# Middle tiles of the key-value sums: from zero-padded full-height products to half-height products inside the projection blocks

## The chip, the cores and the metric

One Trainium2 chip, one NeuronCore. The metric is device time in microseconds (us) of one execution of the whole program. The program does a linear-attention layer and a soft mixture of experts behind it, all in 32-bit floats, in one launch.

## The reference

```python
# attention: batch 8, heads 8, sequence 576, head width 64, 128 features
proj = einsum('bhsd,df->bhsf', x, w_phi)              # x is q or k
proj = proj - max(abs(proj), axis=-1)
phi  = concatenate([exp(proj), exp(-proj)], axis=-1)
kv  = einsum('bhsf,bhsd->bhfd', k_p, v)               # sums over the 576 tokens
z   = sum(k_p, axis=2)
out = einsum('bhsf,bhfd->bhsd', q_p, kv) / (einsum('bhsf,bhf->bhs', q_p, z) + 1e-06)
# soft MoE: x is the attention output as (4608, 512); 32 slots, 8 experts of 4
logits = x @ phi
d = exp(logits - logits.max(0)) / column sums;  slot_input = d.T @ x
slot_out[e] = relu(slot_input[e] @ w1[e]) @ w2[e]
c = exp(logits - logits.max(1)) / row sums;     y = c @ slot_out
```

`kv` and `z` are made together: the kernel gives each row of `v` a 65th column of ones, so that one product gives the 64 columns of `kv` and the column `z`.

## The kernel before, in words

**Units and tiles.** The work of attention is cut into 32 units (`NU`). A unit is one head of a pair of batches: 2 x 576 = 1152 tokens, which make 9 tiles of 128 tokens (`NT`). 576 is four and a half tiles, so tile 4 of each unit, the middle tile, holds the last 64 tokens of one batch in its rows 0 to 63 and the first 64 of the other in rows 64 to 127. The two batches need separate sums.

**Projection blocks.** The tiles of all units in a row are cut into 72 blocks of 4 tiles (`NB`). `proj(b)` (matmuls of line 271) projects the keys of block b into the PSUM tile `psk` and the queries of block b-2 into `psq`. The head width is 64, so each of these matmuls uses 64 rows of the array; key and query products lie in different halves of the rows and alternate in the program: four of each, with 64 x 128 weights and 128 moving columns.

**Behind a projection.** DVE takes the largest absolute value of each key row (`kmax`, line 276), ACT makes two factors of it (`kfac`) and the exponentials `kf` (lines 302 and 305), POOL multiplies `v` with the factors into `vs` (`vals`, line 291). `kvmm` (line 318) then sums `kf` x `vs` over the tiles of a unit into the PSUM tile `kvp`, which has one buffer; its shape is two signs (`pn`) x two batches x 65 columns. Each matmul has 128 rows and 64 weight columns, two of them side by side in the two halves of the array's columns. `kvcopy` (line 327) takes `kvp` out of PSUM. `num` (line 371) multiplies the query exponentials with it, with the same 128 x 64 weights and 65 moving columns; DVE and POOL finish the quotient.

**The middle tile before.** The host stores 10 tiles of `v` for each unit: tile 4 comes twice, once with rows 64 to 127 zero and once with rows 0 to 63 zero. The four matmuls of tile 4 in `kvmm` move 130 columns, both copies, and so add into the sums of both batches at once (`m = 130 if t == 4`, lines 313 to 318). The zero rows keep the batches apart. `place` says where a tile stands in `vs`.

**The rest.** After every head group the tiles of attention output are transposed (line 741), logits are made (line 424) and running slot sums updated. At the end come the two expert layers (lines 848 and 943) and the output (lines 972 to 976). Their weights are 64 tiles of 512 KB, loaded into slots of 4096 bytes per partition. `room` works out how many slots fit beside the working buffers: 26 from the start, and then 29, 35, 38, 40 and 46 as working buffers are closed. The 64 - 46 = 18 last weights go to slots whose first weight has been used.

**The order.** All instructions of the first part are put down by hand, in the order of the string `ORDER`: one letter per task ("c" a projection block, "m" a piece of `kvmm`, "a" and "b" loads), each engine executing its own tasks in that order. `Plan.run` gives a buffer to each task as it comes. All loads and stores are issued by SP, in order; an issue that waits for a free buffer holds up those behind it.

Of the kernel before, what the change touches and what calls it, by code (L numbers as in the profile page):

```python
# [17 lines left out]
FE = 128  # L18
# [6 lines left out]
VW = 10 * 65  # L25
# [19 lines left out]
BUFS = {'xs': 3, 'kf': 3, 'vs': 2, 'vt': 2, 'qf': 3, 'un': 2, 'xT': 4, 'xc': 2}  # L45
PICK = {'xcopy': 'adda', 'kvcopy': 'daad', 'zcopy': 'ada', 'zlt': 'aadaa', 'zde': 'a'}
TOP = 196700


def room(bufs):  # L50

    parts = [bufs["xs"] * XW * 4, bufs["kf"] * 4096 + bufs["vs"] * 2624 + bufs["vt"] * 2624,
             bufs["qf"] * 4096 + 2 * 1056 + 512, bufs["un"] * 2368, (bufs["xc"] + 1) * G * DM * 4]
    return [int(n) // 4096 for n in np.cumsum([TOP - bufs["xT"] * 2048 - sum(parts)] + parts)]


class Plan:
# [42 lines left out]
ORDER = (  # L100
    "abbccdeafdebgbehiejefechigcjdklfmbgdnoelhimjfajkegmhijcpnoclfdmqlrhisgmfjktharujnovmvkbdicnogpcjdwmgwflrjhirqvaw"
    "mxfysbkrkdtnomlhizvnocAwgpvjcjwflmdqbrAArvkshimnoltfwckvdgnojrwfrgdkyjahimzlhivnocwqvpcgbdjmgdflrAfwAhimsjklnotr"
    "hiyAmkcjvnopgwcjbdavmxgzflArdqjmwlAfaAkvrwhisynorhizmtkgcjnovvjpwcblfxdmAqrwAAfsrkgmvhitlnojwkvchwajnoyrblrdiqmv"
    "vgwkzjcdpwfmdrgynoAsrfjkmhilAathiznoAcgvjcvblfxAwmxqdAAwrgpkjsfmnolhirtvmvkwdnorwghijrvyzmAcpjwvcwAbflxyAhrazfAd"
    "imkAlgBnojdBqcCgCjsBbBdatmlCkvjwrnoChirvgfjmhiDkpAnocEwFvcwkflmbhrxqxdimGgsnojBflBtCaxchCjykdiBnozBgCfjmvhwrClpr"
    "vdimDwgvkjwnocEFcblqadHxHIrJIKksfKnoltLmqyAdAgAhirfjmgkhicpjnovscbfvxtwmlwrzflAhrvAAdimwgvhyjrwkdiajrnozvgkmjvcp"
    "nowwcAblfyhAmzqdirlgmkjsfAahrxtnoxmjkvdicAnovApwAgcGlfjhwmlqrJdirfvgmkwjsknoradnotbchijvywcblfxgvmxqjdrwpdhimvgr"
    "kzwAsmkMgylftrnozLAhiAcnojvcbdjawmglfAvrqApjwmkshiArfvtnowmdkMyNvhirwgljrvnojmvczwwpcyAblaAzArdkAlmfAnoBhiBgCcjC"
    "fkdBqdBmCgfjshinoajrlxCAbmktDphivvnocwEgwjclfFrbqrvdmwgBsfBkmktCCjdhiBvnoOajBhiyxCcClrwflrnovNzdmkwhiDgnojpcEqvG"
    "wcFblgsHHrItdmyKIjfzlhiKAdkaxALgmAnoqvJrfMjmgvkwhiwAscnoApctblAxdrjGrgvfwmkdhilrgjvajmvkwnoOPfrjNnomvhicwwPpycyz"  # L110
    "bdkAlmfdgrnojzqJmlAajhixsAfrAOhimtkcnovvpwcgbdjlmgfrwqjdrvAklaAmhixwjnosfchitgmkvbjfxwrlxhrpyvnowmkvczdiAnowqcdy"
# [938 lines left out]
```

## Time and profile before

| what | us |
|---|---|
| three runs of the kernel | 341.21, 337.5, 337.83 (median 337.83) |
| span of the profiled execution | 339.8 |
| PE busy in it | 326.0 |
| DVE, ACT, POOL busy | 243.8, 234.5, 168.3 |
| granted TensorE clock, mean | 0.992 |
| read and written | 63.60 MB, 9.44 MB |

PE is the matmul engine; PEld is the load of its weights, which runs beside the matmuls. Each 32-bit matmul of the program appears twice in the trace, as two passes, each with its own weight load: 1152 matmuls of `num` give 2304 records. Shapes such as "128*64 128x65" are the rows and columns of the array that an instruction uses, then what it moves. The start times of the records tell the rate at which the passes follow each other; their durations (some 0.22 to 0.3 us) hold the way through the array too, so they overlap.

### The profile page before, as it was taken

To read this page: it belongs to the slowest core of one execution; us is meant where nothing else is said; L and a number is where in the kernel's file an instruction comes from. 1 tells how busy PE (TensorE), PEld (TensorE's weight loads), DVE (VectorE), ACT (ScalarE), POOL (GpSimd) and SP (SyncE) were. 2 spreads that over 40 slices of the span, in tenths; PEclk is the share of its full clock that TensorE was granted. 3 is DMA by queue.
4 is the path that set the end of the run, shared out by engine and by line. 5 is a ranking of instruction groups with operands and counts; after the bars stand their busy time and mean duration, and the time that the engine had idled before them with its cause. 6 is when DMAs were issued, how large, how long until landed. Compare 5 with 4: busy or idle time off the path is not lost.

```text
span 339.8 us, 16429 instructions
## 1 busy us (share of the span) xinstructions
PE 326.0 (96%) x6955; PEld 274.8 (81%) x6955; DVE 243.8 (72%) x683; ACT 234.5 (69%) x680; POOL 168.3 (50%) x353
## 2 busy tenths in 40 slices
PE   8999999999999979999999999999999999999981
PEld 4899999999979969999799999979998745356750
DVE  1478888786879877778899887679898652716652
ACT  2899989878876976788788977867886241205541
POOL 1545767773456775642867785148593520240000
PEclk9999999999999999999999999999999999999996
DMA  6647376664656683374467833234617879999987
GB/s 223 182 130 229 103 215 220 182 214 144 247 168 194 200 287 106 106 226 125 167 202 241 291 135 105 66 121 148 212 61 288 301 289 395 408 408 369 395 337 285
DMA packets 22409, 74.10 MB, mean 218 GB/s; under 512 B 2496, under 2 KB 2880, under 8 KB 22336
## 3 DMA queue, kind: packets, MB, share of 16 engines
q1 hardware_dynamic: 22336, 73.05, 62.2%
q8 instruction: 55, 0.90, 1.1%
q14 instruction: 18, 0.15, 0.1%
HBM read 63.60 MB, written 9.44 MB: 215 GB/s over the span
## 4 chain that ended last, share of the span: by engine, by line
PE 88%; DVE 4%; DMA 3%; issue 2%; ACT 1%; POOL 0%; DVEq 0%; ACTq 0%; POOLq 0%
PE kvp L318 23%; PE psn L371 21%; PE psq L271 11%; PE psk L271 10%; PE hp L848 4%; PE psx L741 4%; DMA wt<-w 3%; PE psl L424 3%; PE yp L943 2%; PE pso L972 2%; PE pss L463 2%; PE psw L190 1%; DVE o L973 1%; PE pss L566 1%; PE psd L456 1%
## 5 line engine op out<-in xcount | busy, mean ns | idle before, releaser
L291 POOL TENSOR_TENSOR vs<-vt,mk 128x520 f32<-128x520 f32 (+3 forms) x128 | 91.6, 732 | 72.2 <-ACT mk L280 50.5
L318 PE MATMUL kvp<-vs,kf 128*64 128x65 f32 (+1 forms) x2304 | 92.6, 229 | 0.0
L318 PEld LDWEIGHTS kvp<-vs,kf 128*64 128x64 f32 x2304 | 81.6, 138 | 7.1 <-issue 2.3
L371 PE MATMUL psn<-kvs,qf 128*64 128x65 f32 x2304 | 80.4, 223 | 2.7 <-issue 2.6
L371 PEld LDWEIGHTS psn<-kvs,qf 128*64 128x64 f32 x2304 | 73.6, 138 | 5.9 <-issue 3.7
L271 PE MATMUL psk<-wd,xs 64*128 64x128 f32 x576 | 75.7, 281 | 0.1
L271 PE MATMUL psq<-xs,wd 64*128 64x128 f32 x576 | 75.5, 280 | 0.0
L271 PEld LDWEIGHTS psk<-wd,xs 64*128 64x128 f32 x576 | 67.4, 188 | 3.0 <-issue 1.6
L271 PEld LDWEIGHTS psq<-xs,wd 64*128 64x128 f32 x576 | 67.4, 187 | 2.9 <-issue 1.1
L276 DVE TENSOR_REDUCE mk<-psk 128x4 f32<-128x512 f32 x72 | 48.4, 676 | 16.7 <-PE psk L271 11.2
L333 DVE TRANSPOSE_TENSOR_REDUCE mts<-psq 128x16 f32<-128x512 f32 x72 | 50.7, 707 | 5.7 <-PE psk L271 3.1
L302 ACT ACTIVATE kf<-psk 128x512 f32<-128x512 f32 x72 | 42.6, 593 | 17.5 <-DVE mk L276 7.8
L338 ACT ACTIVATE qf<-psq 128x512 f32<-128x512 f32 x72 | 42.4, 594 | 7.7 <-DVE dn L398 2.2
L382 DVE TENSOR_TENSOR un<-psn,eq 128x195 f32<-128x195 f32 x96 | 33.1, 351 | 18.3 <-PE psn L371 9.6
L413 POOL TENSOR_TENSOR xc<-un,dn 128x256 f32<-128x256 f32 x64 | 39.3, 616 | 13.5 <-DVE dn L398 11.0
L341 ACT ACTIVATE qf<-psq 128x512 f32<-128x512 f32 x72 | 43.2, 603 | 0.5 <-DVE mts L333 0.5
L305 ACT ACTIVATE kf<-psk 128x512 f32<-128x512 f32 x72 | 42.6, 596 | 0.5 <-DVE mk L276 0.4
L387 DVE TENSOR_TENSOR un<-psn,un 128x195 f32<-128x195 f32 x96 | 32.9, 350 | 1.0
L349 ACT ACTIVATE mh<-mts 32x36 f32<-32x36 f32 x128 | 29.5, 231 | 4.6 <-DVE mts L333 2.6
L355 DVE TENSOR_REDUCE eq<-mh 32x9 f32<-32x36 f32 x128 | 26.2, 204 | 1.5
L279 ACT ACTIVATE mk<-mk 128x4 f32<-128x4 f32 x72 | 15.2, 211 | 15.3 <-DVE mk L276 13.8
L973 ACT COPY o<-pso 128x512 f32<-128x512 f32 x20 | 11.4, 597 | 8.9 <-PE pso L972 8.9
(130 smaller groups left out, 346.4 us busy)
## 6 DMA issues: line engine op xcount, KB each, us to landing
wt<-w SPq DMA_DIRECT2D x64, 512.0 KB, 6.5
xs<-xT SPq DMA_DIRECT2D x36, 512.0 KB, 4.3
vt<-vv SPq DMA_DIRECT2D x32, 325.0 KB, 3.3
out<-o SPq DMA_DIRECT2D x17, 512.0 KB, 4.2
out<-o SPq DMA_DIRECT2D x2, 256.0 KB, 4.1
xs<-xT SPq DMA_DIRECT2D x2, 128.0 KB, 2.7
cs<-cst SPq DMA_DIRECT2D x1, 128.5 KB, 3.0
wd<-w SPq DMA_DIRECT2D x1, 64.0 KB, 2.2
```

The source lines that it names most:

```text
L271: nc.tensor.matmul(ps, l, r, start=True, stop=True)
L276: nc.vector.tensor_reduce(km[b][:, 2], kx[b], axis=AX, op=ALU.max, apply_absolute_value=True)
L291: nc.gpsimd.tensor_tensor(vs[b][:, :, place(b, u, t, o):place(b, u, t, o) + n], v[:, t + o:t + o + n].unsqueeze(1).broadcast_to([128, 2, n ...
L302: nc.scalar.activation(kf[b][:, 1], kx[b], AF.Exp, scale=-1.0)
L305: nc.scalar.activation(kf[b][:, 0], kx[b], AF.Exp)
L318: nc.tensor.matmul(ps[f:f + FE // 2, pn, o:o + m], kf[b][:, pn, NT * u + t - 4 * b, f:f + FE // 2], v2[:, pn, at:at + m], start=(t == 0 an ...
L333: nc.vector.tensor_reduce(mts.rearrange("p r j -> p j r")[:, o:o + 4], qx[b].rearrange("p j (r t) -> p (j r) t", t=32), axis=AX, op=ALU.ma ...
L338: nc.scalar.activation(qf[b][:, 0], qx[b], AF.Exp)
L341: nc.scalar.activation(qf[b][:, 1], qx[b], AF.Exp, scale=-1.0)
L371: nc.tensor.matmul(ps[64 * f:64 * f + 64, j, pn], q2[:, pn, 64 * f:64 * f + 64], kv[:, pn, b2], start=True, stop=True)
L382: nc.vector.tensor_tensor(un[u][:, CH * c:CH * c + CH], nx[s][:, :, 0], e[:, 1].unsqueeze(2).broadcast_to([128, CH, 65]), op=ALU.mult)
L413: nc.gpsimd.tensor_tensor(x[:, :, h * D:(h + 1) * D], un[u][:, a:b, 0:64], dn[u][:, a:b].unsqueeze(2).broadcast_to([128, b - a, 64]), op=A ...
```

## The change

Five things change in the code.

1. `v` is stored with 9 tiles per unit, without zeros; `vals` makes one instruction for each piece of a block, and `place` is gone. `vs` has 4 tiles instead of 5.
2. `kvmm` leaves tile 4 out. `proj(b)` does it, three blocks after the block in which the tile lies (`LAG = 3`): four matmuls more, two for each batch, each with 64 rows, 128 weight columns and 65 moving columns. Those of one batch stand at the head of the sequence of one half of the rows, those of the other batch at the tail of the other half's sequence.
3. Both pairs add into the same PSUM bank. So the first matmul of the second pair waits for the last of the first pair, by way of an empty instruction on SP: SP waits for PE, PE waits for SP.
4. The buffers `kf` and `vs` live longer: 4 and 3 of them instead of 3 and 2. `kvcopy` waits for the projection block that holds the middle tile. The ring for software-made DMA descriptors is set to 64 bytes per partition, and `TOP`, the bytes per partition that the kernel plans with, goes from 196700 to 212900. `room` then gives 29, 32, 39, 42, 43 and 49 slots.
5. `ORDER` is a new string.

```diff
-VW = 10 * 65
+VW = NT * 65
+LAG = 3
+VSW = 2 * 4 * 65
-BUFS = {'xs': 3, 'kf': 3, 'vs': 2, 'vt': 2, 'qf': 3, 'un': 2, 'xT': 4, 'xc': 2}
+BUFS = {'xs': 3, 'kf': 4, 'vs': 3, 'vt': 2, 'qf': 3, 'un': 2, 'xT': 4, 'xc': 2}
-TOP = 196700
+TOP = 212900
 ORDER = (
-    "abbccdeafdebgbehiejefechigcjdklfmbgdnoelhimjfajkegmhijcpnoclfdmqlrhisgmfjktharujnovmvkbdicnogpcjdwmgwflrjhirqvaw"
+    "bcaceeefdhbdfigehcieegdckafllhfgjnmdej?kobibjmbhemjncfoipclhgdirdkqgag?rlnjmsjtfmkovnojhvmcw?rp?blamwfvrqwrdij?k"
...
+    middle = {(NT * u + 4) // 4: u for u in range(NU)}
...
+        rows = {0: [], 1: []}
         for i in range(4):
-            two = []
             if b < NB:
-                two.append((kx[b][:, i], x[kh, i], wd[kh]))
+                rows[b % 2].append((kx[b][:, i], x[kh, i], wd[kh]))
             if b > 1:
-                two.append((qx[b - 2][:, i], wd[qh], x[qh, i]))
-            for ps, l, r in two[::-1] if b % 2 else two:
-                nc.tensor.matmul(ps, l, r, start=True, stop=True)
+                rows[1 - b % 2].append((qx[b - 2][:, i], wd[qh], x[qh, i]))
+        u = middle.get(b - LAG)
+        if u is not None:
+            early = 0 if b < NB else b % 2
+            m, at = b - LAG, NT * u + 4 - 4 * (b - LAG)
+            for r in range(2):
+                half_ = half[r]
+                two = [(kvp[u][:, pn, r], kf[m][half_, pn, at], vs[m][half_, pn, at]) for pn in range(2)]
+                rows[r] = two + rows[r] if r == early else rows[r] + two
+        for i in range(max(len(rows[0]), len(rows[1]))):
+            for r in (0, 1):
+                if i < len(rows[r]):
+                    ps, l, m_ = rows[r][i]
+                    mid = l.shape[0] == 64 and m_.shape[-1] == 65
+                    ins = nc.tensor.matmul(ps, l, m_, start=not mid, stop=True, skip_group_check=mid).ins
+                    if mid and r == early:
+                        ahead = ins
+                    elif mid and i + 2 == len(rows[r]):
+                        sync = mybir.DependencyInfo(mybir.DependencyClass.Sync, mybir.DependencyReason.DATA)
+                        relay = nc.sync.nop().ins
+                        tc.add_manual_dep(relay, ahead.name, sync, reason="middle")
+                        tc.add_manual_dep(ins, relay.name, sync, reason="middle")
...
-        for t, n, o in (t0, min(t1, 5) - t0, 0), (max(t0, 4), t1 - max(t0, 4), 1):
-            if n > 0:
-                nc.gpsimd.tensor_tensor(...)
+        g, n = NT * u - 4 * b, t1 - t0
+        nc.gpsimd.tensor_tensor(vs[b][:, :, g + t0:g + t1],
+                                v[:, t0:t1].unsqueeze(1).broadcast_to([128, 2, n, 65]),
+                                km[b][:, 0:2, g + t0:g + t1].unsqueeze(3).broadcast_to([128, 2, n, 65]), op=ALU.mult)
...
-            o, m = 65 * (t > 4), 130 if t == 4 else 65
-            at = 65 * place(b, u, t, 0)
-            for pn in range(2):
+            at = NT * u + t - 4 * b
+            for pn in range(2) if t != 4 else ():
...
-after=[("kvmm", p)]                                    # kvcopy
+after=[("kvmm", p), ("proj", (NT * u + 4) // 4 + LAG)]  # kvcopy
...
-    nc = bacc.Bacc("TRN2", target_bir_lowering=False, num_devices=1)
+    nc = bacc.Bacc("TRN2", target_bir_lowering=False, num_devices=1, dynamic_dma_scratch_size=64)
```

What the new order does to the engines shows at three places. The rows name the line, the operation, what it writes and reads, and the size of what it writes; a bracket names the engines that the row waits for ("Pool_49" is POOL, "DMAHW" a DMA, "SP_sequencer" the empty instruction on SP).

PE around one middle tile, before (line 318 is `kvmm`, line 371 `num`):

```order
L371 MATMUL psn<-kvs,qf 64x65 x12
L318 MATMUL kvp<-vs,kf 64x130 [waits Pool_49]
L318 MATMUL kvp<-vs,kf 64x130 x3
L318 MATMUL kvp<-vs,kf 64x65 x12
L371 MATMUL psn<-kvs,qf 64x65 x12
```

PE around one middle tile now (line 287 is `proj`, line 331 `kvmm`; the rows of line 287 that write `kvp` are the middle tile):

```order
L287 MATMUL kvp<-vs,kf 128x65 [waits Pool_49]
L287 MATMUL psq<-xs,wd 128x128 [waits DMAHW2_49,Activation_49]
L287 MATMUL kvp<-vs,kf 128x65
L287 MATMUL psq<-xs,wd 128x128
L287 MATMUL psk<-wd,xs 128x128 [waits DVE_49]
L287 MATMUL psq<-xs,wd 128x128
L287 MATMUL psk<-wd,xs 128x128
L287 MATMUL psq<-xs,wd 128x128
L287 MATMUL psk<-wd,xs 128x128
L287 MATMUL kvp<-vs,kf 128x65 [waits SP_sequencer_49]
L287 MATMUL psk<-wd,xs 128x128
L287 MATMUL kvp<-vs,kf 128x65
```

The four matmuls that write 64 x 130 are gone, and four that write 128 x 65 stand between the projections; a projection block with a middle tile has 12 matmuls instead of 8. The third of the new four is the one that waits for SP.

PE from one projection block to the next, before:

```order
L271 MATMUL psq<-xs,wd 128x128
L271 MATMUL psk<-wd,xs 128x128
L271 MATMUL psk<-wd,xs 128x128 [waits DMAHW0_49,PE_49,Activation_49]
L271 MATMUL psq<-xs,wd 128x128 [waits Activation_49]
L271 MATMUL psk<-wd,xs 128x128
```

and at a place of the new order:

```order
L287 MATMUL psk<-wd,xs 128x128
L287 MATMUL psq<-xs,wd 128x128
L384 MATMUL psn<-kvs,qf 64x65 [waits DVE_49]
L384 MATMUL psn<-kvs,qf 64x65 x23
L331 MATMUL kvp<-vs,kf 64x65 [waits PE_49,Pool_49]
L331 MATMUL kvp<-vs,kf 64x65 x11
L287 MATMUL kvp<-vs,kf 128x65 [waits Pool_49]
L287 MATMUL psk<-wd,xs 128x128 [waits DVE_49]
```

Before, two blocks mostly follow each other directly (30 unbroken stretches hold two blocks, 12 hold one: 42 stretches); now other products stand between them more often (21 stretches hold two blocks, 30 hold one: 51 stretches).

POOL at the values of a block, before (line 291 is `vals`):

```order
L291 TENSOR_TENSOR vs<-vt,mk 128x2x195 [waits DMAHW2_49]
L291 TENSOR_TENSOR vs<-vt,mk 128x2x130 [waits PE_49,Activation_49]
L291 TENSOR_TENSOR vs<-vt,mk 128x2x195
L413 TENSOR_TENSOR xc<-un,dn 128x4x64 [waits DVE_49]
L291 TENSOR_TENSOR vs<-vt,mk 128x2x130 [waits PE_49,Activation_49,Pool_49]
```

and now (line 312):

```order
L312 TENSOR_TENSOR vs<-vt,mk 128x2x130 [waits PE_49,Activation_49]
L312 TENSOR_TENSOR vs<-vt,mk 128x2x130 [waits DMAHW2_49]
L426 TENSOR_TENSOR xc<-un,dn 128x4x64 [waits DVE_49]
L312 TENSOR_TENSOR vs<-vt,mk 128x520 [waits PE_49,Activation_49]
```

The second copy of the middle tile is gone: 128 instructions of `vals` in all become 96, and 320 tiles become 288.

74 lines of the change are left out of this document (34 added, 40 removed), and 2 rows, old and new, of the table LETTERS.

## The prediction

> **What bounds the kernel now.** I read the page first (engine sums, chain of waits), then the stages in windows, then PE's waits, and last PE's timeline pass by pass. The page's busy line for PE, its chain by engine, and two stages out of the windows:
>
> ```profile
> PE 326.0 (96%) x6955; PEld 274.8 (81%) x6955; DVE 243.8 (72%) x683; ACT 234.5 (69%) x680; POOL 168.3 (50%) x353
> PE 88%; DVE 4%; DMA 3%; issue 2%; ACT 1%; POOL 0%; DVEq 0%; ACTq 0%; POOLq 0%
> 24.00:72.00 48.00, 48.00 (x1260) 46.02 (x1258) 40.07 (x114) 41.17 (x120) 32.85 (x70) 1.00 0.58 181
> 299.00:310.00 11.00, 10.76 (x167) 6.60 (x160) 3.40 (x13) 2.23 (x4) 3.40 (x6) 1.00 1.03 409
> ```
>
> In a window row stand the stretch, its length and PE busy, then PEld, DVE, ACT and POOL, then the granted clock and the share and rate of the DMAs. PE is busy for all 48 us of the second stage, at the full clock, and carries 88% of the chain; DVE and ACT have 7 to 8 us of slack there, POOL 15. The DMAs are full only near the end (1.03 at 409 GB/s), where PE still has work for 10.76 of 11 us. So what counts is how many passes PE issues and at what spacing. PE's longest wait in the stage of attention is one that no engine caused; from PE's waits and the waits of its weight loads:
>
> ```profile
> PE psn L371 <- issue: 2.6, 1, 2.6
> PEld kvp L318 <- POOL vs L291: 0.8, 1, 0.8
> ```
>
> That single 2.6 us gap lies inside a run of equal matmuls, so I take it for something that this execution had by chance. Without it the span would be 339.8 - 2.6 = 337.2, next to the median run of 337.83. I make the sum as a difference and add it to the median.
>
> **What the padded middle tile costs.** PE's timeline (start, duration, group):
>
> ```profile
> 101.74 1.15 PE L318 MATMUL kvp<-vs,kf 128*64 128x65 f32 x32
> 102.72 1.57 PE L371 MATMUL psn<-kvs,qf 128*64 128x65 f32 x48
> 104.12 1.31 PE L318 MATMUL kvp<-vs,kf 128*64 128x130 f32 x32
> 105.26 1.58 PE L371 MATMUL psn<-kvs,qf 128*64 128x65 f32 x48
> ```
>
> Starts count, not durations. 48 passes of 65 columns take 104.12 - 102.72 = 1.40 us, 0.0292 each (two run side by side, so a pair steps by 0.0583). The next 32 passes take 1.14 us and are a mixture: 8 of 130 columns and 24 of 65. 24 x 0.0292 = 0.70, so the 8 wide ones take 0.44, 0.055 each. With 32 units, **the removed passes are worth 32 x 0.44 = 14.1 us** on the path.
>
> **What the half-height passes will cost.** Nothing in this trace has 64 x 128 weights and 65 moving columns, so the price is bounded from both sides. The upper neighbour is the projection itself (same weights, 128 moving columns), the lower one is 65 columns behind 64-column weights. The starts of one projection block, and of the next visit to projections with what follows it:
>
> ```profile
> 99.93 0.27 PE L271 MATMUL psq<-xs,wd 64*128 64x128 f32 x1
> 100.04 0.27 PE L271 MATMUL psq<-xs,wd 64*128 64x128 f32 x1
> 100.60 0.27 PE L271 MATMUL psq<-xs,wd 64*128 64x128 f32 x1
> 107.00 0.37 PE L271 MATMUL psq<-xs,wd 64*128 64x128 f32 x1
> 108.99 0.92 PE L318 MATMUL kvp<-vs,kf 128*64 128x65 f32 x24
> ```
>
> From 99.93 to 100.60 are six steps of one half of the rows: 0.112 each; the other half steps beside it. A middle tile adds four passes to each half (two matmuls, two passes each). At 65-column spacing that is 4 x 0.0583 = 0.233 us, at projection spacing 4 x 0.112 = 0.447. Which one holds is the question of the case, and weight loads answer it. Their durations by shape, and the one group that has wide weights and few moving columns, with the group behind it:
>
> ```profile
> L318 PEld LDWEIGHTS kvp<-vs,kf 128*64 128x64 f32 x2304 | 81.6, 138 | 7.1 <-issue 2.3 <-POOL eq L358 1.0 <-POOL vs L291 0.8
> L271 PEld LDWEIGHTS psq<-xs,wd 64*128 64x128 f32 x576 | 67.4, 187 | 2.9 <-issue 1.1 <-ACT mk L280 0.2
> L943 PEld LDWEIGHTS yp<-wt,sh 128*32 128x32 f32 x384 | 10.6, 110 | 5.6 <-issue 3.1
> L611 PEld LDWEIGHTS pst<-sf,acc 128*128 128x128 f32 x8 | 1.0, 191 | 0.0
> 280.40 1.08 PE L611 MATMUL pst<-sf,acc 128*128 128x32 f32 x8
> 281.32 0.31 PE L633 MATMUL psc<-cs,xT 128*128 128x128 f32 x1
> ```
>
> A load takes 110, 138 and 187 to 191 ns for 32, 64 and 128 weight columns, and 64 rows load no faster than 128 (187 against 191). And in L611 eight passes with 128 weight columns and only 32 moving columns take 281.32 - 280.40 = 0.92 us, 0.115 each: as long as a projection pass. So a pass with 128 weight columns steps at the pace of its load, however few columns move. I take 0.112. **The added passes are worth 32 x 0.447 = 14.3 us**, and array time stays as it was: +0.2 us. Each pass moves half as many columns as before, but loads weights twice as wide, and that is what counts.
>
> **Visits to the projection shape.** A change of array shape costs a start. 107.00 to 108.99 is a stretch with two blocks: 1.99 us for 16 steps of 0.112 (1.79), so 0.20 per visit. The new order makes 51 visits instead of 42: +1.8 us. Against that, the 128 x 32 shape (L424 and others) is entered 15 times instead of 17 before the expert layers:
>
> ```profile
> 79.50 1.01 PE psl L424 x32
> 261.76 0.79 PE psl L424 x24
> ```
>
> Eight passes make 0.22 us, so 24 make 0.66 of the 0.79: 0.13 per visit, -0.3 us. Visits together: **+1.5 us**.
>
> **The relay over SP.** New waits: in each of 32 units the first matmul of the late pair waits for SP, which waits for PE. Queued behind it on PE are the last key or query product, the other late matmul and all that follows, so a late relay costs the path its whole delay; DVE and ACT then wait for that block's maxima and exponentials. How long a hop takes: the end of a projection block and the load that it released, and SP's own instructions at that line.
>
> ```profile
> 61.83 0.27 PE L271 MATMUL psq<-xs,wd 64*128 64x128 f32 x1
> 62.17 0.33 SPq L178 DMA_DIRECT2D xs<-xT  x1
> L178 SPq EVENT_SEMAPHORE  x27: 17/17/28, 4.8 to 238.3; - x27
> ```
>
> 61.83 + 0.27 = 62.10 to 62.17: 0.07 for a hop from PE to SP. There and back with SP's 0.02 is some 0.16 us. The first pair's last pass starts three steps into the block and ends at 3 x 0.112 + 0.27 = 0.61. The late pair's load is due after seven steps of its own half, 0.78. So 0.17 us are there and 0.16 are needed. Bounds: nothing per unit, or 0.2 us if the way back is slow: 0 to 6.4 us in all. I take 0.01 per unit, +0.3 us. SP is in order, and spends much time in front of loads that aren't free yet:
>
> ```profile
> SPq L178 <- PE psk L271: 105.4, 25, 10.1
> SPq L182 <- POOL vs L291: 55.6, 17, 6.2
> ```
>
> That would be fatal if such a load stood right ahead of a relay. In the new order at least 31 matmuls stand between the last load and the relay (1.8 us at 0.058), and what the loads wait for stands ahead of that again. I price it at nothing; if that cover is gone, one 0.33 us issue per unit is 10 us.
>
> **Edits without a price.** POOL loses a tile and an instruction per unit. The four shapes of `vals`:
>
> ```profile
> L291 POOL TENSOR_TENSOR vs<-vt,mk 128x520 f32<-128x520 f32 x32 | 33.8, 1057 | 27.3 <-ACT mk L280 20.4 <-PE pss L463 5.7 <-PE kvp L318 0.9
> L291 POOL TENSOR_TENSOR vs<-vt,mk 128x130 f32<-128x130 f32 x32 | 13.0, 405 | 11.5 <-ACT mk L280 5.7 <-PE kvp L318 5.5
> ```
>
> Three tiles more cost 0.652 us, so a tile is 0.217 and an instruction 0.188: 32 x 0.405 = 13 us less for POOL. But PE waited 0.8 us for `vs` in the whole run, so at most that comes out; I count nothing. 10% fewer bytes of `v`, more buffers, a smaller descriptor ring (all loads and stores are SP's) and three more weight slots move transfers that hide under a full PE; if the weights were late, three slots would be worth up to three loads of 512 KB at 409 GB/s, 3.8 us, but the last window before the output shows PE working while they land. The later `kvcopy` is covered too: between the middle tile's block and the next unit's first sum stand 0.7 us or more of other PE work, as before.
>
> **Sum.** -14.1 + 14.3 + 1.5 + 0.3 = +2.0 us, less about 0.3 for the last block, where the middle tile fills an idle half of the rows: +1.7. **Forecast 337.8 + 1.7 = 339.5 us**, no change by the measure of this kernel, where runs tell about 1% (3.4 us) apart. Its own range is 337 to 342.
>
> **Rivals.**
>
> *Price by moved columns (faster).* If a half-height pass steps at 0.0583, the tile costs 32 x 0.233 = 7.5 instead of 14.3 us: 332.7 us. For it speaks that two passes of 65 columns fit the same pace in 128 x 64; against it L611. The Trainium skill, TensorE: Matmul & The Clock Gate, section "Back-to-back issue gap", prices an isolated matmul by its moving columns alone, N/2.4 + 2.5 ns, and would give this rival's price; the 0.0292 us per pass of 65 columns agrees with it, L611's 0.115 doesn't, and the same section warns that weight loads set the spacing too. Chance 0.15.
>
> *The new order closes gaps (faster).* What is left of PE's gaps is about 3 us without the 2.6; all of it gone, and POOL's 0.8, gives 339.5 - 3.8 = 335.7 us; with some of the rival above, past 1%. Chance 0.07.
>
> *The relay is late (slower).* One mechanism: the late pair waits for SP's way back. At 0.15 us per unit it costs 4.8 us: 344.0. It decides from 0.06 us per unit (1.9 us on top of the forecast passes 1%). For it speaks the margin of 0.01 us; against it that PE holds issued passes in hand. Chance 0.19.
>
> *Loads don't hide behind a matmul in the same rows (slower).* Then a half-height pass is a load and a matmul one after the other, 0.112 + 0.058 = 0.170: 32 x 4 x 0.170 = 21.8 us instead of 14.3: 347.0. The same page's Part 3 says that a load overlaps a running matmul only in other rows. The 65-column passes speak against it: load and matmul in the same rows would take twice their 0.058 step. Chance 0.03.
>
> **How the numbers follow.** Forecast 0.56; faster 0.15 + 0.07 = 0.22; slower 0.19 + 0.03 = 0.22. The range runs from 332.5, which takes in the price by columns, to 344.0, a relay 0.15 us late.
>
> **What would show it.** A block with a middle tile takes 12 steps of 0.112 (1.34 us and the 0.20 of a visit), the half-height passes 0.11 apart; 51 visits; no idle PE ahead of the late pair; POOL 13 us less busy without gain. A step of 0.06 in those passes, PE busy some 7 us shorter, or a gap of over 0.05 us ahead of the matmul that waits for SP would prove it wrong.

## The result, and the profile after

The change makes the kernel slower: 349.52 us (median of four runs, 348.21 to 350.03) beside 339.07 for the kernel before on the same chip, a ratio of 1.031 (95% interval 1.0276 to 1.0344). Over all the runs that follow, the kernel before stood at 338.6, 0.8 us above the median of three on which the forecast was built. A few executions of the runs below fell into a slower state; their medians leave these out. The forecast was 339.5, so 10 us are missing, and the time lies outside the range (332.5 to 344.0). The profiled execution took 349.12 with a span of 347.2, at a clock of 0.995.

The page of the changed kernel: busy line, chain by engine, and the two groups of the half-height passes (`kvp` written in line 287).

```profile
PE 329.2 (95%) x6955; PEld 276.5 (80%) x6955; DVE 247.2 (71%) x683; ACT 235.7 (68%) x680; POOL 156.9 (45%) x321
PE 77%; DVE 9%; DMA 6%; ACT 3%; issue 3%; POOL 1%; SPq 0%; DVEq 0%; ACTq 0%; POOLq 0%
L287 PE MATMUL kvp<-vs,kf 64*128 64x65 f32 x256 | 38.2, 269 | 0.0
L287 PEld LDWEIGHTS kvp<-vs,kf 64*128 64x128 f32 x256 | 33.4, 187 | 3.1 <-issue 1.7
```

Busy times are nearly those of before; what changed is the chain. PE carries 77% of it instead of 88%, DVE 9 instead of 4, the DMAs 6 instead of 3. The half-height matmuls themselves waited for nothing (0.0 in the last column). One block with a middle tile, from PE's timeline (start, duration):

```profile
70.83 0.32 PE L287 MATMUL kvp<-vs,kf 64*128 64x65 f32 x1
71.00 0.27 PE L287 MATMUL kvp<-vs,kf 64*128 64x65 f32 x1
71.11 0.27 PE L287 MATMUL kvp<-vs,kf 64*128 64x65 f32 x1
71.22 0.27 PE L287 MATMUL kvp<-vs,kf 64*128 64x65 f32 x1
71.33 0.32 PE L287 MATMUL psk<-wd,xs 64*128 64x128 f32 x1
...
71.72 0.27 PE L287 MATMUL psq<-xs,wd 64*128 64x128 f32 x1
...
71.84 0.33 PE L287 MATMUL kvp<-vs,kf 64*128 64x65 f32 x2
...
72.01 0.27 PE L287 MATMUL kvp<-vs,kf 64*128 64x65 f32 x1
72.12 0.27 PE L287 MATMUL kvp<-vs,kf 64*128 64x65 f32 x1
...
72.37 0.85 PE L331 MATMUL kvp<-vs,kf 128*64 128x65 f32 x21
```

In each half of the rows the half-height passes step by 0.11 us, the pace of a projection pass, as forecast. The visit takes 72.37 - 70.83 = 1.54 us: twelve steps and 0.20. There is no idle time ahead of the late pair: it starts at 71.84, 0.12 behind the last query product of its half (71.72). So the price on PE was right. The loads tell another story. What SP waited for (total, times, longest):

```profile
SPq L292 <- PE kvp L287: 179.5, 32, 10.4
SPq L181 <- PE psk L287: 18.9, 6, 5.0
```

Before, SP's long waits (105.4 us) were for the buffers of its own loads. Now it stands 179.5 us at line 292, the relay, up to 10.4 us at a time, and the loads behind it stand too. The relay of the block at 70.83, and what SP issues behind it:

```profile
71.66 0.33 SPq L185 DMA_DIRECT2D vt<-vv  x1
72.04 0.90 SPq L245 DMA_DIRECT2D wt<-w  x2
73.04 0.38 SPq L185 DMA_DIRECT2D vt<-vv  x1
73.51 0.39 SPq L181 DMA_DIRECT2D xs<-xT  x1
```

The `xs` buffer of the last row had been free since 63.2 (the end of the PE instruction that this load waits for). It is issued 10.3 us later, behind four other loads that the relay had held too, and shares the DMAs with them. The chain of waits and PE's timeline show the end of it, in this order:

```profile
72.44 1.07 PE kvp L331 x31
73.51 7.38 DMA xs<-xT
80.89 0.04 issue
```

```profile
79.80 0.43 PE L287 MATMUL kvp<-vs,kf 64*128 64x65 f32 x2
80.94 0.37 PE L287 MATMUL psq<-xs,wd 64*128 64x128 f32 x1 [0.70 <-DMA xs<-xT]
```

The load takes 7.4 us and PE stands for it, in the middle of a block. Worked out in the same way for 34 `xs` loads, the time from free buffer to issue was 0.07 us (median) and 0.69 (mean) before, and 5.45 and 5.45 now, at most 16.7. PE's waits for `xs`, which were none before:

```profile
PE psq L287 <- DMA xs<-xT: 1.5, 2, 0.8
PE psk L287 <- DMA xs<-xT: 0.9, 2, 0.5
```

Counted by start times against the regular steps, these places cost 4 us in all, and so can't be all of 10.9. Three theories went into the experiments. **Theory 1**: the relay holds up the loads behind it on SP. **Theory 2**: gaps of PE, without any wait in the records, that end 2.3 to 2.5 us behind the start of an instruction fetch (4.4 us in this execution, 3.0 in that of before; the last section shows one). **Theory 3**: the new order makes PE wait for ScalarE (ACT), VectorE (DVE) and GpSimd (POOL), apart from any relay.

### The profile page after: what moved, and what is told of

The parts are those of the page before. It is cut to its first block, busy times and chain, and to the rows that moved or that the text cites. A ratio compares the mean times of both kernels' runs of the same rounds, so it can differ in the third digit from the quotient of the medians.

```text
span 347.2 us, 16372 instructions
## 1 busy us (share of the span) xinstructions
PE 329.2 (95%) x6955; PEld 276.5 (80%) x6955; DVE 247.2 (71%) x683; ACT 235.7 (68%) x680; POOL 156.9 (45%) x321
## 4 chain that ended last, share of the span: by engine, by line
PE 77%; DVE 9%; DMA 6%; ACT 3%; issue 3%; POOL 1%; SPq 0%; DVEq 0%; ACTq 0%; POOLq 0%
PE psn L384 17%; PE kvp L331 15%; PE psk L287 9%; PE psq L287 8%; DMA xs<-xT 6%; PE kvp L287 5%; PE psx L760 4%; PE yp L962 4%; PE hp L867 4%; PE psl L437 2%; PE pso L991 2%; PE psw L193 1%; DVE mts L346 1%; DVE o L992 1%; PE pss L476 1%
## 5 line engine op out<-in xcount | busy, mean ns | idle before, releaser
L312 POOL TENSOR_TENSOR vs<-vt,mk 128x520 f32<-128x520 f32 (+3 forms) x96 | 79.7, 837 | 49.0 <-ACT mk L303 36.8
L287 PE MATMUL psq<-xs,wd 64*128 64x128 f32 x576 | 78.4, 281 | 1.5 <-DMA xs<-xT 1.5
L287 PE MATMUL psk<-wd,xs 64*128 64x128 f32 x576 | 78.2, 281 | 1.5 <-DMA xs<-xT 0.9
L331 PE MATMUL kvp<-vs,kf 128*64 128x65 f32 x2048 | 71.7, 223 | 2.3 <-issue 1.5
L287 PEld LDWEIGHTS psq<-xs,wd 64*128 64x128 f32 x576 | 68.5, 187 | 4.9 <-DMA xs<-xT 1.8
L287 PEld LDWEIGHTS psk<-wd,xs 64*128 64x128 f32 x576 | 68.4, 188 | 3.7 <-issue 1.4
L331 PEld LDWEIGHTS kvp<-vs,kf 128*64 128x64 f32 x2048 | 65.2, 138 | 5.8 <-issue 2.9
L346 DVE TRANSPOSE_TENSOR_REDUCE mts<-psq 128x16 f32<-128x512 f32 x72 | 50.8, 708 | 10.9 <-PE psq L287 6.4
L287 PE MATMUL kvp<-vs,kf 64*128 64x65 f32 x256 | 38.2, 269 | 0.0
L287 PEld LDWEIGHTS kvp<-vs,kf 64*128 64x128 f32 x256 | 33.4, 187 | 3.1 <-issue 1.7
```

Source lines behind the costliest of these rows:

```text
L287: ins = nc.tensor.matmul(ps, l, m_, start=not mid, stop=True, skip_group_check=mid).ins
L312: nc.gpsimd.tensor_tensor(vs[b][:, :, g + t0:g + t1], v[:, t0:t1].unsqueeze(1).broadcast_to([128, 2, n, 65]), km[b][:, 0:2, g + t0:g + t1] ...
L331: nc.tensor.matmul(kvp[u][f:f + FE // 2, pn, t > 4], kf[b][:, pn, at, f:f + FE // 2], vs[b][:, pn, at], start=(t == 0 and pn == 0), stop=( ...
L346: nc.vector.tensor_reduce(mts.rearrange("p r j -> p j r")[:, o:o + 4], qx[b].rearrange("p j (r t) -> p (j r) t", t=32), axis=AX, op=ALU.ma ...
```

## Experiments

All times are medians; the ratio is to the kernel before on the same chip.

| run | order | middle tile | relay | us | ratio, 95% |
|---|---|---|---|---|---|
| (before) | old | padded | none | 338.6 | 1 |
| (change) | new | halves | SP | 349.5 | 1.028 to 1.034 |
| no_relay | new | halves | none | 343.38 | 1.010 to 1.015 |
| pool_relay | new | halves | POOL | 344.58 | 1.012 to 1.021 |
| hoist | new, xs loads earlier | halves | SP | 347.54 | 1.016 to 1.030 |
| hoist2 | new, xs and vt loads earlier | halves | SP | 349.24 | 1.030 to 1.037 |
| before_relay | old | padded | idle, SP | 338.69 | 0.998 to 1.003 |
| order_padded | new | padded | none | 343.26 | 1.013 to 1.021 |
| order_padded_relay | new | padded | idle, SP | 349.55 | 1.031 to 1.036 |
| old_order | old | halves | SP | 351.72 | 1.033 to 1.041 |
| old_pool_relay | old | halves | POOL | 355.01 | 1.047 to 1.062 |
| old_no_relay | old | halves | none | 345.71 | 1.011 to 1.027 |
| old_late_end | old | halves | none | 345.93 | 1.014 to 1.028 |
| no_mid2 | new | left out | none | 335.82 | 0.986 to 0.993 |
| before_nomid | old | left out | none | 336.51 | 0.990 to 0.998 |
| half_mid | new | half of the halves | none | 343.06 | 0.999 to 1.022 |
| before_half | old | half of the padded | none | 338.15 | 0.996 to 1.000 |
| slots | old | padded, 49 slots | none | 338.38 | 0.996 to 1.001 |

### The relay

**no_relay.**

```diff
-two = [(kvp[u][:, pn, r], kf[m][half_, pn, at], vs[m][half_, pn, at]) for pn in range(2)]
-rows[r] = two + rows[r] if r == early else rows[r] + two
+two = [(kvp[u][:, pn, r] if r == early or not rows[r] else rows[r][0][0][:, 0:65], kf[m][half_, pn, at], vs[m][half_, pn, at]) for pn in range(2)]
+rows[r] = two + rows[r]
...
-relay = nc.sync.nop().ins
```

> Edit: the relay on SP is taken out. So that nothing has to be ordered, the late pair of each middle block writes into the first projection's own bank of its half instead of the shared kvp bank, and the projection behind it overwrites it: the sums of one batch's half of each middle tile are left out, every matmul stays where and as long as it was. Theory 1 (the relay waits in SP's in-order queue and holds the xs loads behind it): the time from a buffer's release to the issue of its xs load falls from a median of 5.45 us to under 0.2 us as in the kernel before, TensorE's waits for xs loads fall from about 4 us to under 1 us, and the time falls by 4 to 7 us, to 343 to 345.5. Theory 2 (gaps of TensorE 2.3 to 2.5 us behind instruction fetches): the loads issue early all the same but the time stays within 1 us of 349.5. Theory 3 (the new order makes TensorE wait for ScalarE, VectorE and GpSimd): also within 1 us, with waits on those engines where they were.

343.38, 6.1 us less than the change. The edit takes more out than the wait: the late pair moves to the head of its half and no longer writes `kvp`. The median hold of an `xs` load fell to 0.07 us, as theory 1 had it (the mean to 2.4), and the waits for `xs` went from PE's list. SP now waits for the buffers of its own loads:

```profile
SPq L185 <- POOL vs L305: 103.9, 24, 7.7
SPq L181 <- PE psk L287: 64.8, 18, 8.0
```

Theory 2 falls as the main cause, but it may have a part: the two profiled executions lie 349.12 - 343.37 = 5.75 us apart, and the gaps of theory 2 are 4.4 us in the one and 1.5 in the other. One profile of each kernel can't tell whether the relay brings such gaps. And 4.7 us to the kernel before are left. A second run, no_mid, was meant to leave the middle tiles out; its kernel came out the same as this one, so it only repeats it: 343.01.

> Edit: the change without its middle tiles: the 128 half-height passes of 65 columns and the relays are left out (all sums of the middle tiles are missing), the projections, the order and everything else stay. It prices the half-height passes. By the weight loads of 128 columns (4 passes of 0.11 us for each middle) it is 32 x 0.44 = 14.1 us below the run without the relay: 329.3, within 1 us. By the moved columns alone (half of that) 336.4.

**hoist** and **hoist2.** In front of a block with a middle tile, the next `xs` load (in hoist2 the next `vt` load too) is taken out of the order's later part when its buffer is free by the order's own count.

```diff
-        for letter in ORDER:
+        todo, b = list(ORDER), 0
+        while todo:
+            letter = todo.pop(0)
+            if letter == "c":
+                while (b - LAG) in self.middle and self.tokens["xs"] and "b" in todo and self.done.issuperset(self.tasks["load"][0][2]):
+                    todo.remove("b")
+                    todo[0:0] = ["c"]
+                    letter = "b"
+                    break
+                else:
+                    b += 1
```

> Edit: all of the change stays, result complete; where a projection block with a middle tile is next in the order and a load's buffer is free by the order's own count, that xs load is put ahead of the block, so that it stands ahead of the relay in SP's queue. Theory 1: the loads that stood behind a relay now issue at their buffer's release or wait there for less; the hold falls from a mean of 5.45 us to about 1 us, TensorE's 4 us of waits for loads mostly vanish, and the time is 343 to 347. Theories 2 and 3: 348.5 to 350.5, no change.

> Edit: as the run hoist, and the value loads (vt) are put ahead of the block with the middle tile in the same way; result complete. In hoist the xs loads were held for 0.4 us on average, but a vt load still stood behind a relay and TensorE waited 2.7 us for GpSimd and it at 256.8. Theory 1: with neither kind of load behind a relay, 343.5 to 346. If the vt load's own wait for GpSimd, now ahead of the relay, makes the relay late, TensorE waits at the late pairs and the time is 347 to 352.

hoist gave 347.54, half a us above what theory 1 allowed; hoist2 gave 349.24. In hoist the `xs` loads are held for 0.40 us on average, and PE waits for no `xs` any more; but the value loads are still behind a relay. SP's queue and POOL in the profile of hoist:

```profile
245.46 0.38 SPq L191 DMA_DIRECT2D xs<-xT  x1
251.28 0.80 SPq L195 DMA_DIRECT2D vt<-vv  x2
```

```profile
256.14 2.43 POOL L322 TENSOR_TENSOR vs<-vt,mk 128x260 f32<-128x260 f32 x3 [5.41 <-DMA vt<-vv]
```

POOL stands 5.4 us for `vt`, and PE behind it. With the `vt` loads in front as well (hoist2), SP waits for POOL there and comes to the relay late. PE's waits in hoist2:

```profile
PE kvp L301 <- SPq L306: 3.4, 5, 1.0
```

This is the rival that its expectation named. SP takes its queue in order, and neither of the two places served both: with the loads behind the relay the loads are late, with the loads ahead of it the relay is.

**pool_relay** has the relay on GpSimd.

```diff
-relay = nc.sync.nop().ins
+relay = nc.gpsimd.nop().ins
```

> Edit: the change with its relay on GpSimd's queue instead of SP's; result complete. Theory 1: xs loads issue within 0.2 us of their buffer's release again and TensorE's waits for loads fall under 1 us; GpSimd's queue is held in their place, up to 16 times the 5 us for which a relay stands there, ahead of vs scalings of 2.4 us; with GpSimd busy 157 of 347 us this hides for the most part: 342 to 347. If GpSimd's held scalings are late instead, the waits reappear as TensorE's waits for vs and the time is 348 to 352. Theories 2 and 3: no change, 348.5 to 350.5.

344.58, 4.9 us less than the change and 1.2 more than without any relay. POOL is held now, but with some 157 us of work in 345 it hides most of that:

```profile
POOL xn L426 <- PE kvp L287: 10.2, 4, 3.6
POOL vs L312 <- PE kvp L287: 5.6, 7, 1.6
```

**before_relay** and **order_padded_relay** add an idle relay to padded passes, in the old and in the new order. Nothing on PE waits for it.

```diff
-                nc.tensor.matmul(ps, l, r, start=True, stop=True)
+                ins = nc.tensor.matmul(ps, l, r, start=True, stop=True).ins
+                if i == 1 and b - 3 in middle:
+                    relay = nc.sync.nop().ins
+                    sync = mybir.DependencyInfo(mybir.DependencyClass.Sync, mybir.DependencyReason.DATA)
+                    tc.add_manual_dep(relay, ins.name, sync, reason="middle")
```

> Edit: the kernel before with one thing of the change added: in each projection block that stands where the change has its middle tile, SP runs a no-operation that waits for the second pair of the block's projections on TensorE; nothing waits for that no-operation. TensorE's work and the order are those of before. Theory 1: the xs loads behind it are held for a mean of some 5 us instead of 0.69, and the time rises by 2 to 5 us, to 341 to 344. Theories 2 and 3: no change, within 1 us of the kernel before.

> Edit: as the run order_padded, with an idle no-operation on SP in each projection block that stands where the change has its middle tile, waiting for the second pair of the block's matmuls; nothing on TensorE waits for it. Theory 1 (what a relay costs is the loads queued behind it on SP): xs loads are held for a mean of about 5 us, TensorE waits for them, and the time is 4 to 6 us above order_padded, 347 to 349 if that stands at 343. If the cost lies in the late pair's wait for its relay on TensorE, the idle one costs nothing and the two agree within 1 us. Then the idle relay that cost nothing in the order of before is no special case of that order.

In the old order the idle relay costs nothing (338.69): a miss of theory 1 as I had put it. There the `xs` load behind a relay mostly waits for a buffer that comes free no earlier than the relay itself (relays done at 61.81 and 81.31 us, buffers free at 62.24 and 82.63), and the mean hold stays near 0.7 us. In the new order the same idle relay costs 349.55 - 343.26 = 6.3 us. What SP and PE waited for in order_padded_relay:

```profile
SPq L274 <- PE psq L272: 92.0, 14, 15.4
SPq L274 <- PE psk L272: 54.3, 11, 6.2
```

```profile
PE psk L272 <- DMA xs<-xT: 2.0, 2, 1.3
PE psq L272 <- DMA xs<-xT: 1.4, 1, 1.4
```

No matmul waits for this relay, so its price comes from what it holds up on SP. Theory 1 holds in the new order, with the condition that the order puts loads behind the relay whose buffers are already free. How much of the 6 us are PE's waits for these loads, and how much the gaps of theory 2, stays open.

### The order and the middle tile

**order_padded** is the kernel before in the order of the change, with its buffer counts and slots. To make room, two small rings of statistics have two buffers instead of three.

```diff
-BUFS = {'xs': 3, 'kf': 3, 'vs': 2, 'vt': 2, 'qf': 3, 'un': 2, 'xT': 4, 'xc': 2}
+BUFS = {'xs': 3, 'kf': 4, 'vs': 3, 'vt': 2, 'qf': 3, 'un': 2, 'xT': 4, 'xc': 2}
 ORDER = (
-    "abbccdeafdebgbehiejefechigcjdklfmbgdnoelhimjfajkegmhijcpnoclfdmqlrhisgmfjktharujnovmvkbdicnogpcjdwmgwflrjhirqvaw"
+    "bcaceeefdhbdfigehcieegdckafllhfgjnmdej?kobibjmbhemjncfoipclhgdirdkqgag?rlnjmsjtfmkovnojhvmcw?rp?blamwfvrqwrdij?k"
...
```

> Edit: the kernel before, with its padded 130-column passes and no relay, run in the order of the change, with the change's buffer counts and 49 weight slots; result complete (two small rings of statistics are one buffer shorter to make room). It prices the new order alone. Theory 3 (the order itself costs TensorE waits for ScalarE, VectorE and GpSimd, and nine more projection visits 1.8 us): the change without its relay stood at 343.4 against 338.6, and halves and padded passes cost TensorE the same 0.44 us, so this comes out near 343, within 1 us. If instead the order is free and the halves cost what is left, it comes out within 1 us of the kernel before, 338.6.

343.26: the new order with padded passes is as slow as with halves and no relay. I took that for 5 us that the order costs in itself, and expected the old order to be rid of them.

**old_order** is the reverse: all of the change but its order.

```diff
 ORDER = (
-    "bcaceeefdhbdfigehcieegdckafllhfgjnmdej?kobibjmbhemjncfoipclhgdirdkqgag?rlnjmsjtfmkovnojhvmcw?rp?blamwfvrqwrdij?k"
+    "abbccdeafdebgbehiejefechigcjdklfmbgdnoelhimjfajkegmhijcpnoclfdmqlrhisgmfjktharujnovmvkbdicnogpcjdwmgwflrjhirqvaw"
...
```

> Edit: the change with its halves, its relay on SP, its buffer counts and its 49 weight slots, but in the order of before (a step that is not yet ready there is put off until it is: three kvs copies move by one place; three weight loads are added); result complete. It takes the new order alone out of the change. Theory of the two parts (halves and padded passes cost TensorE the same 0.44 us a middle; the new order costs 5 us by its own waits and 6 more because its loads stand behind relays, and in the order of before an idle relay held nothing): within 1.5 us of the kernel before, 338 to 340. If the halves or the real relay cost something in any order: 342 to 349.

351.72, 13 us above the kernel before. The theory of two separate parts fell: halves are not neutral in the old order, though PE steps through them at the same pace. **old_no_relay** (no_relay's edit in that order) splits the 13 us, and two runs that leave the middle tiles out tell what each of them is worth.

> Edit: as the run old_order (halves in the order of before), but without the relay: as in no_relay, the late pair of each middle goes into its half's own projection bank and is overwritten, so one batch's sums of each middle tile are left out. Theory A (in that order the halves themselves cost: 0.44 us more of TensorE in a projection block makes what ScalarE and VectorE wait for late, and TensorE then waits for them, while the passes taken out of the kvp runs had stood where nobody waited): 347 to 352, near old_order's 351.7. Theory B (the real relay costs in every order, by the loads of values and weights behind it and by the late pair's wait): 338 to 341, near the kernel before.

**no_mid2**, against no_relay:

```diff
-                rows[r] = two + rows[r]
+                rows[r] = rows[r]
```

> Edit: the change without its middle tiles, as was meant for the run no_mid, whose kernel had come out the same as that of no_relay (it stands as a repeat of it: 343.0 beside 343.4): the 128 half-height passes of 65 columns and the relays are left out (all sums of the middle tiles are missing), the projections, the order and everything else stay. By the weight loads of 128 columns it is 32 x 0.44 = 14.1 us below the run without the relay: 329.1, within 1 us. By the moved columns alone (half of that) 336.2. If part of TensorE's freed time turns into waits for the other engines, in between: 331 to 335.

**before_nomid**, against the kernel before:

```diff
-            for pn in range(2):
+            for pn in range(2) if t != 4 else ():
```

> Edit: the kernel before without its padded passes: the 128 passes of 130 columns are left out (all sums of the middle tiles are missing), all else stays. It prices what the change removes. If TensorE's busy time is the time, as the prediction's sum had it: 32 x 0.44 = 14.1 us less, 324 to 325. If ScalarE and VectorE bound what TensorE frees, as in no_mid2, where 14.1 us of half-height passes taken out brought 7.4: 328 to 334.

With the four variants in both orders:

| | left out | padded | halves, no relay | halves, relay on SP |
|---|---|---|---|---|
| old order | 336.5 | 338.6 | 345.7 | 351.7 |
| new order | 335.8 | 343.3 | 343.4 | 349.5 |

PE's work for a middle tile is 14.1 us in all padded and halves cells. It shows as 2.2 us (padded, old order), 9.2 (halves, old order), 7.4 and 7.6 (new order). Without middle tiles the two orders are alike, so the new order costs nothing in itself: what differs is how much of the middle's work each one hides. The theory that stands after this: PE, ACT and DVE wait for each other all through the attention stage, and 14.1 us of PE's work can be taken out with hardly any gain, because PE then waits for ACT and DVE. The page of before_nomid, and PE's and its weight loads' waits in it:

```profile
PE 316.0 (95%) x6699; PEld 263.5 (79%) x6699; DVE 241.7 (72%) x683; ACT 233.6 (70%) x680; POOL 167.9 (50%) x353
PE 72%; DVE 9%; ACT 7%; DMA 6%; issue 2%; POOL 1%; ACTq 0%; DVEq 0%; SPq 0%; POOLq 0%
```

```profile
PE psq L271 <- ACT qf L341: 2.0, 6, 0.4
PE psn L371 <- DVE un L387: 0.6, 2, 0.4
```

```profile
PEld psq L271 <- ACT qf L341: 3.3, 8, 0.6
```

None of these rows was there before. Each wait is short, 0.6 us at most, and PE still counts as busy for 95%: a matmul of 0.27 us covers the idle time behind it, so gaps of 0.2 us don't show in a busy share. They show in the start times. From PE's first matmul to the first `hp` (the first expert layer), before_relay (the kernel before with idle relays, and without the chance gap) needs 277.9 us and before_nomid 274.8. The `kvp` runs fall from 74.1 to 61.6 us, and 2.8 come back in `psn` (`num`), 3.6 in the projections, 2.2 at changes of shape and 0.5 in `psx` (the transposes). Not all of these 9.1 us are waits for ACT and DVE: gaps behind instruction fetches sum to 3.7 us in the profile of before_nomid and to 0.2 in that of before_relay. Counted roughly by start times, the passes that a signal of ACT or DVE released late take some 5 to 6 us more than in before_relay. So the theory has rows for the larger part of what came back, not for all of it. The halves lie in projection blocks, whose results ACT and DVE wait for. That this place is why they cost 7 us more than the padded passes in the old order fits the numbers, but no run moved them elsewhere. The change also has `kvcopy` wait for the block with the middle tile, while `kvp` has one buffer; no run tells the two apart.

**half_mid** and **before_half** leave out half of the middle's work.

```diff
-... vs[m][half_, pn, at]) for pn in range(2)]
+... vs[m][half_, pn, at]) for pn in range(1)]
```

```diff
-            for pn in range(2):
+            for pn in range(1 if t == 4 else 2):
```

> Edit: the run no_relay with one of the two matmuls of each half's middle pair left out (half of the half-height passes, and the late pair's sums as in no_relay, are missing): a middle adds 0.22 us to TensorE's block, the cost that the change's own plan gives it, instead of 0.44. Without any middle the new order took 335.8, with all of it and no relay 343.2 to 343.4. Theory P (the new order was fitted to 0.22 us a middle, and what goes beyond is what shows): 336 to 338. Theory L (each part of the work shows alike, half of it half): 339 to 340.5.

> Edit: the kernel before with half of its padded passes left out (one sign of each middle tile's sums is missing): 0.22 us less of TensorE for each middle, 7.05 us in all. Without any padded pass it took 336.5 against 338.6. If the order of before covers the padded passes evenly: 337 to 338. If TensorE's busy time counted up to some point: below 335 cannot be, since none at all gave 336.5; a time within 0.5 us of either end tells where the cover begins.

338.15 in the old order, 0.2 above the first case, with an interval up to no change: too little to tell where the cover begins. In the new order 343.06 with an interval of 0.999 to 1.022: no gain that can be measured, and no theory confirmed, since three runs lie up to 5 us apart. The profiled one, 343.06, is full of PE's gaps without a releaser:

```profile
PE kvp L324 <- issue: 3.4, 3, 1.3
PE psn L377 <- issue: 1.3, 2, 0.7
PE psq L287 <- issue: 1.2, 1, 1.2
```

They make 5.9 us, where no_relay, at 343.37, had 0.9 in such rows. Without them half of the halves would show as some 5 us, nearer theory P than theory L, but one execution is too little to tell. That the new order was fitted to 0.22 us a middle is not shown.

### What the relay costs in the old order

There it cost 351.72 - 345.71 = 6.0 us too, though `xs` loads were held for under 0.1 us only (median).

**old_pool_relay** puts that relay on GpSimd:

> Edit: as the run old_order (halves in the order of before), with the relay on GpSimd's queue instead of SP's; result complete. With the relay on SP it took 351.7, without it 345.7, though xs loads were held for a median of 0.08 us only. If those 6 us come from what SP's queue holds behind the relay or from SP reaching the relay late (0.8 us at 90 us): 345 to 347.5. If they come from the relay's round trip and the late pair's place at the block's end, which any queue keeps: 350 to 352.

**old_late_end**, against old_no_relay:

> Edit: as the run old_no_relay (halves in the order of before, no relay), with the late pair at the end of its block again, where the change has it: it repeats 65 columns of its half's last projection twice, into the same place, so one batch's sums of each middle tile are left out as there. If the relay's 6 us in the order of before are the late pair's place (the kvs copy, which waits for it, and what waits for that copy come later): near old_order's 351.7, 349.5 to 352. If they are the wait for the relay itself: near old_no_relay's 345.7, 344.5 to 347.

```diff
-                rows[r] = two + rows[r]
+                if r != early and rows[r]:
+                    o, l, m_ = rows[r][-1]
+                    two = [(o[:, 0:65], l, m_[:, 0:65])] * 2
+                rows[r] = two + rows[r] if r == early else rows[r] + two
```

On GpSimd it is no better (355.01; the profiled execution, 352.2, stays within 1.4 us of old_order's all the way), so taking the relay off SP's queue brings nothing here. That GpSimd's own held work costs the same by chance is not excluded. With the late pair at its place but no relay it is 345.93, so it isn't the place in PE's order either. What is left is the wait itself, or the kvs copy: in old_late_end the late pair doesn't write `kvp`, so that copy doesn't wait for it. The second is not excluded. In old_order PE waited for that copy:

```profile
PE psn L402 <- DVE kvs L358: 1.1, 2, 0.6
```

and 1.8 of the drift between the two profiles lie at waits of this kind, 0.8 at one late relay, some 2 at gaps without a visible wait. Why the relay costs 6 us in the old order stays open.

### The weight slots

**slots** is the kernel before with the smaller ring and 49 slots; four more weight loads stand in its order.

```diff
-TOP = 196700
+TOP = 212900
...
-    nc = bacc.Bacc("TRN2", target_bir_lowering=False, num_devices=1)
+    nc = bacc.Bacc("TRN2", target_bir_lowering=False, num_devices=1, dynamic_dma_scratch_size=64)
```

> Edit: the kernel before with the smallest scratch ring and 49 weight slots instead of 46 alone (four more of the weight loads go into the main stage); halves and order of before. The stage from the first hp matmul to the end was 57.8 us before and 56.0 with the change. If the slots brought that: 1 to 2 us below the kernel before, 336 to 337.5. If it was three transposes (psc) that the new order took ahead of hp: within 0.5 us of it. If the added loads get in the way of xs loads: 339 to 341.

338.38, the time of the kernel before (338.55 on the same chip). The slots bring nothing; the stage from the first `hp` matmul to the end took 57.5 us in it, 57.9 before and 56.1 with the change. The shorter end therefore is not the slots'; order_padded, with the new order, has it too (56.3). No kernel that computes everything was measurably faster than the kernel before.

## Why the prediction was wrong, point by point

**The first step that failed** is the one on which the sum stands: "So what counts is how many passes PE issues and at what spacing." It took 96% busy and 88% of the chain for a bound, and gave each us of PE's work one us of time. The "-14.1" for the removed passes measured 2.2 us (before_nomid; 0.8 to 3.4 by its interval), the "+14.3" for the added ones 7.6 in the new order and 9.2 in the old. The two don't cancel: instead of +0.2 they come to +7.1 in the old order (338.6 to 345.7). The slack of ACT and DVE that I read from a window ("7 to 8 us" of 48) was a sum over the window; the new waits of before_nomid come one at a time, at most 0.6 us each.

**The second** is the relay: "I price it at nothing; if that cover is gone, one 0.33 us issue per unit is 10 us." I looked at what stands ahead of the relay on SP and at PE's own wait, and named what is queued behind the waiting matmul on PE, but not what is queued behind the waiting relay on SP: the loads. Its term of 0.3 us measured 6.1 (no_relay) and, by itself, 6.3 (order_padded_relay). The rival "the relay is late" had the right sign and the wrong mechanism: it forecast a gap ahead of the late pair, and there was none. The row with SP's 105.4 us of waits, which the prediction quoted, could have raised the question what one more wait on SP does to the loads behind it.

**The third** is the order. The prediction took PE's gaps as unchanged under a new order and counted visits alone (+1.5). With padded passes the new order costs 4.7 us (order_padded), with middle tiles left out it costs nothing (335.8 beside 336.5): here the price of an order hung on the work in it, and couldn't be told apart from that.

By the runs the sum is -2.2 (padded passes out), -0.7 (new order), +7.6 (halves), +6.1 (relay) = +10.8; measured 349.5 - 338.6 = 10.9. The runs form a chain from the one kernel to the other, so that the terms add up proves nothing; by way of the old order they are -2.1, +9.2 (halves), +6.0 (relay) and -2.2 (new order).

The base was low too. The prediction put a span without its gap (337.2) beside a time (337.83). The time of that execution without the gap is 341.21 - 2.6 = 338.6, where the later runs of the kernel lie.

**What was right**: the price of a half-height pass on PE (0.112 forecast, 0.11 measured). The Trainium skill's page TensorE: Matmul & The Clock Gate, section "Back-to-back issue gap", has a formula for an isolated matmul; worked out from it, an estimate of the spacing is 65/2.4 + 2.5 = 29.6 ns. This trace disagrees for weights of 128 columns: with both halves of the rows at work a pass starts every 0.055 us. It agrees with the same section's caution that weight loads set the spacing. How long a load takes is not a matter of its columns alone, as the prediction has it: in the same trace the transposes of line 741 load 128 columns in 141 ns. Right too were 51 visits, POOL less busy by 11.4 us (13 forecast) without gain, and slots without gain. But the rivals "price by moved columns" and "gaps closed" would have needed the same first step.

## What to carry to other kernels

Take the work out before you price it: a run that leaves the passes out shows what they are worth on the path, and here it was 2 us of 14. Before an instruction that waits is put on a queue that also issues loads, list what stands behind it there, and how long before its use each of those loads has to be issued. The same work can cost 2 us in one order and 7 in another, so an order and the work in it have to be measured together; whether a new search of the order would win the difference back was not tried.

## What the runs showed of the hardware

PE stops now and then without any wait in the records, and goes on 2.0 to 2.6 us behind the start of an instruction fetch on queue q8 (55 fetches, 0.90 MB, so 16 KB each). The largest one stands in the profile of before, in a run of equal matmuls; the fetch starts at 125.1:

```profile
124.34 0.63 PE L371 MATMUL psn<-kvs,qf 128*64 128x65 f32 x14
127.56 0.51 PE L371 MATMUL psn<-kvs,qf 128*64 128x65 f32 x10 [2.58 <-issue]
```

Such gaps sum to 0.2 us (before_relay), 0.5 (slots), 1.5 (no_relay), 3.0 (before), 3.7 (no_mid2, before_nomid), 4.4 (the change) and 5.8 (half_mid) in one execution each. The Trainium skill's page Runtime: NRT & Kernel Launch, section "Instruction fetch mechanics", has blocks of 16 KiB and calls the cost of crossing one mostly hidden; the size agrees with the trace, and most of the 55 crossings are hidden, but single ones took up to 2.8 us. What decides which ones are hidden was not tried.
